# One head's output-projection rows in three DMAs ahead of the last V loads of a two-problem decode-attention kernel

## The chip, the cores and the metric

The kernel runs on one core of a Trainium2 chip. The core has five engines with an instruction stream each: TensorE (PE; its weight loads are listed as PEld), VectorE (DVE), ScalarE (ACT), GpSimd (POOL) and SyncE (SP). SP does no arithmetic here: it issues DMAs, transfers between the chip's memory (HBM) and the core's SBUF. Sixteen DMA engines carry them out. The metric is the device time of one execution in microseconds (us), as a median of several runs; less is better.

## The reference

Two independent problems, A and B, of the same sizes, each one step of attention with a cache and a window. Batch 2, one query token, 32 query heads, 16 key/value heads, head size 128, model width 576. Of 16,384 cached positions the last 4,096 are used.

```python
q = (x @ wq).reshape(B, Sq, Hq, Dh).transpose(0, 2, 1, 3)
k = jnp.repeat(k_cache[:, :, Sk - W:, :], rep, axis=1)      # W = 4096, rep = 2
v = jnp.repeat(v_cache[:, :, Sk - W:, :], rep, axis=1)
scores = jnp.einsum("bhqd,bhkd->bhqk", q, k) * (Dh ** -0.5)
p = softmax(scores, axis=-1)
o = jnp.einsum("bhqk,bhkd->bhqd", p, v)
return o.transpose(0, 2, 1, 3).reshape(B, Sq, Hq * Dh) @ wo
...
jnp.concatenate([a, b], axis=-1)
```

All tensors are bfloat16. The windows of K and V of both problems are 134 MB, wq and wo some 19 MB more; every byte is read once.

## The kernel before

**Staging.** K and V come in slabs of 4,096 KB: 128 partitions of 32 KB, four pairs of batch and key/value head at a time. There are eight slabs of K and eight of V in each problem, 16 pairs (steps) in all. They pass through `ring`, a buffer of four slots (NR = 4). A slab's load (L256) may be issued when the last reader of the slab four places earlier in the order is done: for K the last of the four DVE transposes (L515), for V the last of PE's products with the softmax weights (L631).

**One step.** DVE transposes the K slab in four parts into `xt`, PE multiplies each with the queries (L540), DVE, PE and ACT make the maximum and the exponential, PE multiplies the weights with the V slab into ACC, and ACT copies ACC out. Two steps make a group; the normed head outputs of a group are multiplied with their rows of wo, which lie in the SBUF buffer `wob`. Groups 0 to 3 belong to A, 4 to 7 to B; `proj[7]` is the projection of A's last group.

**The order.** It is written out in Python as lists of operations, one list for each engine; an operation names those that it depends on, and the needed semaphore waits are worked out from that. All loads but one are issued by SP, in the order of `stream`. Its last entries are K of step 13, V of 12, K of 14, K of 15, V of 13, V of 14 and V of 15. An issue that has to wait holds back every later one of SP. A transfer is cut into rows, one packet for each, and each DMA engine works through its own rows in the order of the issues. A load is complete when its semaphore has counted 16.

**The end.** The last slab, V of step 15, is loaded in two pieces (PIECES, L249 to L253) of 96 and 32 of its 128 column blocks, 3,072 KB and 1,024 KB, each with a semaphore of its own. Then `issue_wo(3)` loads the rows of wo for B's last group: 576 KB for step 14 (L291), and through `issue_last` (L272 to L279) the rows of the four heads of step 15. A head has 128 rows of 576 numbers, 1152 bytes each: 144 KB. HEADS, `[(0, 1), (2,), (3,)]`, groups them into three transfers: heads 0 and 1 in one of 288 KB, head 2, head 3. They have the semaphores wl0, wl1 and wl2. Then come the two outputs (L831), of two rows each; A's needs no wait there, B's waits for the end.

PE's work for step 15 after the last piece: the V product, three products whose result is not used, the sum over column blocks (L678), the projection of step 14's heads (L790 with `Rsb`), and that of step 15's heads (L790 with `oTn`), two halves of 288 columns for each head, in the order of HEADS:

```python
parts = [([(oTn[:, h, :], 4 + h) for h in hs], [norm[D_], wo_last[n_]], False, False, n_ == len(HEADS) - 1)
         for n_, hs in enumerate(HEADS)]
```

So the products of heads 0 and 1 wait for DVE's norm (L719) and wl0, those of the next entry for wl1, and the last for wl2. Then ACT and DVE copy the sums into the output row (L822, L823), SP issues the output and waits for it.

Of the kernel before, what the change touches and what calls it, by code (L numbers as in the profile page):

```python
# [59 lines left out]
def build_kernel(nc, probs, out, cfg=None):  # L60
# [8 lines left out]
    NPROB = len(probs)  # L69
# [19 lines left out]
    HH = HD // 2  # L89
# [11 lines left out]
    assert NPROB == 2 and GPP == 4 and NG == 8  # L101
    NSW = 32
    unit_of = {G: u for u, (g0, n) in enumerate(UNITS) for G in range(g0, g0 + n)}
    HEADS = [(0, 1), (2,), (3,)]
    NPC = len(PIECES)

    def by_group(G):
# [6 lines left out]
    with es:  # L114
# [3 lines left out]
        wob = sb("wob", [128, NSW, NOUT], BF16)  # L118
# [62 lines left out]
        x_sem = sem("xload")  # L181
        wl_sem = [sem("wl%d" % n_) for n_ in range(len(HEADS))]
        out_sem = sem("outdone")
# [12 lines left out]
        def dma_op(eng, sem_h, n_dmas, fn, deps, tag):  # L196
            op = S.add(eng, fn, deps, tag)
            dma_count[sem_h] = dma_count.get(sem_h, 0) + 16 * n_dmas
            op.dma = (sem_h, dma_count[sem_h])
            return op  # L200
# [30 lines left out]
        reader = {}  # L231
        wq_dma = {}
        wo_dma = {}
        wo_last = []
        qproj = {}
        proj = {}
        nxt = [0]

        def issue_slab(n):
            kind, D_ = stream[n]  # L240
            if kind == "Q":
                issue_wq(n, D_)
                return
            P, g = D_ // SPP, D_ % SPP
            src_t = probs[P][1] if kind == "K" else probs[P][2]
            src = src_t.rearrange("b h s d -> (b h) s d")[g::SPP, Sk - W:Sk, :].rearrange("c (r j) d -> r c (j d)", r=32)
            r = n % NR
            deps = [reader[n - NR]] if n >= NR else []
            if n == len(stream) - 1:  # L249
                for n_, (ja, jb) in enumerate(PIECES):  # L250
                    def fq(e, n_=n_, ja=ja, jb=jb):
                        return e.dma_start(ring[:, r, ja * 128:jb * 128], src[:, :, ja * 128:jb * 128]).then_inc(piece_sem[n_], 16)  # L252
                    pieces.append(dma_op("sp", piece_sem[n_], 1, fq, deps, "%s%d_q%d" % (kind, D_, n_)))  # L253
                issue_wo(3)
                return
            slab_dma[n] = dma_op("sp", ring_sem[r], 1, lambda e: e.dma_start(ring[:, r, :], src).then_inc(ring_sem[r], 16),  # L256
                                 deps, "%s%d" % (kind, D_))

        def issue_wq(n, P):
            wqP = probs[P][3]  # L260
            r = n % NR
            deps = [reader[n - NR]] if n >= NR else []
            wq_dma[P] = dma_op("sp", wq_sem, 1, lambda e: e.dma_start(
                wqr[:, P, :], wqP[NFC * 128:D, :].rearrange("r (h n) -> r h n", h=2)).then_inc(wq_sem, 16), [], "wqr%d" % P)
            slab_dma[n] = dma_op("sp", ring_sem[r], 1, lambda e: e.dma_start(
                ring[:, r, :], wqP[0:NFC * 128, :].rearrange("(p s) n -> p (s n)", s=NFC)).then_inc(ring_sem[r], 16), deps, "wq%d" % P)

            if P == 0:
                for P_ in range(1, NPROB):
                    x_dma[P_] = load_x(P_, "sp")  # L270

        def issue_last(woP, lo, r0, deps):  # L272
            for n_, hs in enumerate(HEADS):
                def f(e, n_=n_, hs=hs):
                    t, r = divmod(hs[0], 2)
                    row = t * HH + r0 + 256 + 128 * r
                    return e.dma_start(wob[:, lo + 4 + hs[0]:lo + 4 + hs[0] + len(hs), :],
                                       woP[row:row + 128 * len(hs), :].rearrange("(h d) n -> d h n", d=128)).then_inc(wl_sem[n_], 16)
                wo_last.append(dma_op("sp", wl_sem[n_], 1, f, deps, "wl%d" % n_))  # L279

        def issue_wo(part):
            lo, n, r0, P, deps, Gs = (
                (0, 32, 0, 0, [qkeep.get(NG - 1)], (0, 1, 2, 3)),
                (0, 16, 0, 1, [proj.get(3)], (4, 5)),
                (16, 8, 1024, 1, [proj.get(5)], (6,)),
                (24, 4, 1536, 1, [proj.get(7)], (7,)))[part]
            assert None not in deps
            woP = probs[P][4]
            sem_ = wo_sem[lo // 16]
            src = woP.rearrange("(t r) n -> t r n", t=2)[:, r0:r0 + 64 * n, :].rearrange("t (p s) n -> p t (s n)", s=n)  # L290
            op = dma_op("sp", sem_, 1, lambda e: e.dma_start(  # L291
                wob[:, lo:lo + n, :].rearrange("p s n -> p (s n)"), src).then_inc(sem_, 16), deps, "wo%d" % part)
            for G in Gs:
                wo_dma[G] = op
            if part == 3:
                issue_last(woP, lo, r0, deps)

        def issue_until(n_needed):
            while nxt[0] <= n_needed:
                for part in w_at.pop(stream[nxt[0]], []):  # L300
                    issue_wo(part)
                issue_slab(nxt[0])
                nxt[0] += 1
# [462 lines left out]
        def do_proj(D_):  # L766
# [10 lines left out]
            else:  # L777
                parts = [([(oTn[:, h, :], 4 + h) for h in hs], [norm[D_], wo_last[n_]], False, False, n_ == len(HEADS) - 1)
                         for n_, hs in enumerate(HEADS)]
            for lhs, deps, start, rstart, rstop in parts:  # L780
# [146 lines left out]
        for e in ENGS:  # L927
            n = 0
# [63 lines left out]
def bass_concat_heads__sliding_block_cached__sliding_block_cached__decode_kernel(  # L992
    nc, A_x, A_k_cache, A_v_cache, A_wq, A_wo, B_x, B_k_cache, B_v_cache, B_wq, B_wo, out,
):
    build_kernel(nc, [(A_x, A_k_cache, A_v_cache, A_wq, A_wo), (B_x, B_k_cache, B_v_cache, B_wq, B_wo)], out)
# [28 lines left out]
```

## Time and profile before

| | us |
|---|---|
| median of 3 runs (lowest to highest) | 362.61 (362.55 to 362.83) |
| the profiled execution | 363.02 |
| its span, first to last instruction | 361.8 |
| PE busy | 218.6 |
| DVE busy | 200.9 |
| ACT busy | 68.2 |
| POOL busy | 35.3 |
| wo rows of step 14 (L291): issued, landed | 330.1, 358.3 |
| heads 0 and 1 (wl0): issued, landed | 330.7, 359.0 |
| head 2 (wl1): landed | 359.4 |
| head 3 (wl2): issued, landed | 331.9, 359.7 |

The span is the time between the first and the last instruction of the profiled execution. Its whole time is some 1.2 us longer, as the metric includes what lies around the program. No compute engine is busy for more than 60% of the span, while 153.1 MB are read at a mean of 423 GB/s. The end of the profiled execution, in order of time (start, length, engine, line, operation, output and input; in brackets the idle time of the engine before it, and what ended it):

```profile
356.87 0.61 PE L631 MATMUL acc<-ring,pC 128*32 128x512 bf16 x8 [1.01 <-DMA ring<-in_B_v_cache_dram]
...
358.55 0.17 DVE L719 TENSOR_TENSOR oTn<-tb,rsb 128x8 bf16<-128x8 f32 x1 [3.51 <-PE tb L678]
359.07 0.12 PEld L790 LDWEIGHTS st<-wob,oTn 128*2 128x2 bf16 x4 [0.29 <-DVE oTn L719]
359.10 0.94 PE L790 MATMUL st<-wob,oTn 128*2 128x288 bf16 x8
359.40 0.08 PEld L790 LDWEIGHTS st<-wob,oTn 128*2 128x2 bf16 x2 [0.22 <-DMA wob<-in_B_wo_dram]
359.75 0.08 PEld L790 LDWEIGHTS st<-wob,oTn 128*2 128x2 bf16 x2 [0.27 <-DMA wob<-in_B_wo_dram]
360.08 0.40 ACT L822 ACTIVATE pR<-st 2x288 bf16<-2x288 f32 x1 [1.88 <-PE st L790]
```

Besides instructions the trace holds every packet of the DMA engines (start, length, size, queue, but not the engine's number) and the times at which each semaphore was raised. A load of 128 rows raises its semaphore 16 times, once for each DMA engine that is done with its share; such a time is called a mark below. A transfer has landed with its last mark.

### The profile page before, as it was taken

What the parts mean: (1) busy time and instruction counts of PE and PEld (TensorE: products, weight loads), DVE (VectorE), ACT (ScalarE), POOL (GpSimd) and SP (SyncE); (2) the same over time, 40 slices, a digit from 0 to 9 for tenths busy, and PEclk for the clock granted to TensorE, in tenths of its full rate; (3) what the DMA queues carried; (4) which work ended last, traced back from release to release, by engine and by line L of the source; (5) the groups of instructions that cost most, each with busy time, mean ns of one, the idle gap of its engine ahead of it and who ended that gap; (6) DMA issues with size and microseconds to landing.
All of it is one profiled execution on the core that took longest, in us unless ns stands there. A gap on an engine that the chain in (4) does not pass through costs nothing.

```text
span 361.8 us, 2730 instructions
## 1 busy us (share of the span) xinstructions
PE 218.6 (60%) x1318; PEld 55.8 (15%) x945; DVE 200.9 (56%) x175; ACT 68.2 (19%) x149; POOL 35.3 (10%) x55
## 2 busy tenths in 40 slices
PE   0399195763747207466574737766867707657786
PEld 0010021120111101112120201212121201211132
DVE  4112599846647019283756658392919239079931
ACT  1036502130203002103020203020201203002131
POOL 1000000004000400001300040002100040200020
PEclk9999689997889857969698978899898978969999
DMA  8999999999999999999999999999999999999996
GB/s 348 421 449 406 464 406 437 431 408 453 415 442 438 428 424 438 429 428 438 417 446 422 435 428 442 426 435 428 424 424 440 431 424 433 431 438 428 438 409 248
DMA packets 6491, 153.27 MB, mean 424 GB/s; under 512 B 712, under 2 KB 1232, under 8 KB 1616
## 3 DMA queue, kind: packets, MB, share of 16 engines
q1 hardware_dynamic: 6476, 153.10, 98.8%
q8 instruction: 9, 0.15, 0.2%
q14 instruction: 2, 0.02, 0.0%
q10 hardware_dynamic: 4, 0.00, 0.0%
HBM read 153.10 MB, written 0.00 MB: 423 GB/s over the span
## 4 chain that ended last, share of the span: by engine, by line
DMA 72%; DVE 17%; PE 7%; ACT 3%; SPq 1%; issue 0%
DMA ring<-in_B_k_cache_dram 34%; DMA ring<-in_A_k_cache_dram 27%; DVE xt L515 14%; DMA wob<-in_B_wo_dram 8%; DMA wob<-in_B_x_dram 3%; PE st L188 3%; PE st L540 3%; ACT wob L465 1%; DVE wob L475 1%; ACT qk L483 1%; PE st L450 1%; DVE m L550 1%; ACT wob L470 1%; DVE nM L563 0%; SPq L252 0%
## 5 line engine op out<-in xcount | busy, mean ns | idle before, releaser
L515 DVE STREAM_TRANSPOSE xt<-ring 128x2048 f32<-128x2048 f32 x64 | 145.3, 2284 | 86.6 <-DMA ring<-in_A_k_cache_dram 49.8
L540 PE MATMUL st<-xt,zq 128*128 128x512 bf16 x256 | 111.6, 436 | 122.6 <-DVE xt L515 98.1
L188 PE MATMUL st<-xt,zq 128*128 128x512 bf16 x256 | 110.1, 430 | 0.0
L540 PEld LDWEIGHTS st<-xt,zq 128*128 128x128 bf16 x256 | 27.1, 106 | 216.3 <-DVE xt L515 113.5
L631 PE MATMUL acc<-ring,pC 128*32 128x512 bf16 x512 | 32.5, 381 | 1.2 <-DMA ring<-in_B_v_cache_dram 1.2
L568 ACT ACTIVATE nMrep<-nM 1x128 f32<-1x128 f32 x16 | 4.9, 308 | 146.9 <-DVE nM L563 146.9
L643 ACT ACTIVATE acc_sb<-acc 128x512 bf16<-128x512 f32 x16 | 9.5, 596 | 79.9 <-PE acc L631 79.9
L593 DVE STREAM_TRANSPOSE pC<-pR 128x1024 bf16<-128x1024 bf16 x16 | 19.6, 1223 | 3.7 <-ACT pR L585 2.1
L650 POOL TENSOR_TENSOR acc_sb<-acc_sb,masks 128x1024 bf16<-128x1024 bf16 (+1 forms) x8 | 13.4, 1679 | 66.6 <-ACT acc_sb L643 66.6
L550 DVE TENSOR_REDUCE m<-st 128x1 f32<-128x1024 f32 x16 | 19.0, 1190 | 1.4 <-PE st L188 1.4
L502 POOL TENSOR_TENSOR zq<-qk,masks 128x128 bf16<-128x128 bf16 x16 | 6.3, 398 | 136.2 <-PE st L188 114.4
L585 ACT ACTIVATE pR<-st,bias_sb 128x1024 bf16<-128x1024 f32 x16 | 17.8, 1114 | 0.5
L475 DVE STREAM_TRANSPOSE wob<-wob 128x512 f32<-128x512 f32 x8 | 5.7, 711 | 20.3 <-ACT wob L465 12.9
L415 ACT ACTIVATE st<-maskB 128x1024 f32<-128x1024 bf16 x16 | 16.5, 1032 | 1.6 <-POOL rsel L600 0.4
L786 PE MATMUL ot<-wob,Rsb 128*2 128x512 bf16 x56 | 15.2, 390 | 0.0
L631 PEld LDWEIGHTS acc<-ring,pC 128*32 128x32 bf16 x512 | 12.4, 96 | 15.9 <-issue 3.2
L600 POOL TENSOR_TENSOR rsel<-masks,rsum 128x16 f32<-128x16 bf16 x8 | 1.7, 216 | 108.0 <-ACT pR L585 108.0
L188 PE MATMUL tb<-wob,Rsb 128*2 128x64 bf16 x56 | 10.9, 195 | 0.0
L375 PE MATMUL tb<-wob 4*128 4x16 bf16 x5 | 0.3, 179 | 14.5 <-DVE wob L380 14.5
L653 POOL TENSOR_TENSOR acc_sb<-acc_sb 128x512 bf16<-128x512 bf16 (+1 forms) x8 | 8.2, 1029 | 0.6
L188 PE MATMUL st<-ring,wob 128*128 128x512 bf16 x24 | 7.9, 445 | 0.0
L579 ACT ACTIVATE bias_sb<-tb 128x1 f32<-128x1 f32 x16 | 2.7, 171 | 24.8 <-PE tb L573 24.8
(89 smaller groups left out, 99.5 us busy)
## 6 DMA issues: line engine op xcount, KB each, us to landing
ring<-in_A_k_cache_dram SPq DMA_DIRECT2D x8, 4096.0 KB, 30.4
ring<-in_A_v_cache_dram SPq DMA_DIRECT2D x8, 4096.0 KB, 32.5
ring<-in_B_k_cache_dram SPq DMA_DIRECT2D x8, 4096.0 KB, 28.4
ring<-in_B_v_cache_dram SPq DMA_DIRECT2D x7, 4096.0 KB, 32.8
wob<-in_A_wo_dram SPq DMA_DIRECT2D x1, 4608.0 KB, 43.3
ring<-in_A_wq_dram SPq DMA_DIRECT2D x1, 4096.0 KB, 12.7
ring<-in_B_wq_dram SPq DMA_DIRECT2D x1, 4096.0 KB, 22.6
ring<-in_B_v_cache_dram SPq DMA_DIRECT2D x1, 3072.0 KB, 25.5
```

The lines of the kernel that those rows point to most:

```text
L188: return e.add_instruction(mybir.InstMatmult(name=nc.get_next_instruction_name(), engine=i.engine, ins=[e.lower_ap(rhs), i.ins[1]], outs=[ ...
L415: chain[(s, "fill")] = S.add("act", lambda e: e.activation(ST[s % 2][:, :].rearrange("k (h j) -> k h j", h=2), maskB[:].unsqueeze(1).broad ...
L475: chain[(G, "qtr")] = S.add("dve", lambda e: e.transpose(qtr[:].bitcast(FP32), qrow[:].bitcast(FP32)), evs, "qtr%d" % G)
L515: Xop[(s, u)] = S.add("dve", lambda e: e.transpose(xt[:, i % NKT, :].rearrange("k (j w) -> k j w", w=64), ring[:, n % NR, :].bitcast(FP32) ...
L540: first = last = e.matmul(bank, zq[:, p4, s % NZQ, w0:w0 + 128], mv, start=False, stop=stop, skip_group_check=True)
L550: chain[(s, "max")] = S.add("dve", lambda e: e.tensor_reduce(m1[:, 0:1], ST[s % 2][:, :], AX.X, ALU.max), d, "max%d" % s)
L585: chain[(s, "exp")] = S.add("act", lambda e: e.activation(pR[:, :], ST[s % 2][:, :], ACTF.Exp, bias=bias_sb[:, 0:1], scale=SCALE, accum_ou ...
L593: chain[(s, "pC")] = S.add("dve", lambda e: e.transpose(pC[:, s % NPT, :, :].rearrange("k j c -> k (j c)"), pR[:, :]), d, "pC%d" % s)
L631: last = e.matmul(ACC[32 * cb:32 * cb + 32, 0:512], pC[:, D_ % NPT, j0_:j0_ + 4, :].rearrange("k j c -> k (j c)"), ring[:, n % NR, j0_ * 1 ...
L643: acc_ev[D_] = S.add("act", lambda e: e.activation(acc_sb[:, D_ % 2, :], ACC[:, :], ACTF.Copy), d, "accev%d" % D_)
L650: t = S.add("pool", lambda e: e.tensor_tensor(v, v, maskJ[:].unsqueeze(1).unsqueeze(3).broadcast_to([128, l1 - l0, 4, 128]), ALU.mult), [a ...
L786: first = e.matmul(OT[0:Bb, 0:NB0], l_, wob[:, w0 + s_, 0:NB0], start=start and begin, stop=end, skip_group_check=True)
```

## The change

HEADS becomes `[(0, 1), (3,), (2,)]`: the second transfer of step 15's heads is now head 3, the third head 2, and PE multiplies in that order. Head 3's 128 rows are no longer one transfer after V. They come in three, of rows 0 to 14, 14 to 65 and 65 to 128 (SHARES: 14, 51 and 63 rows), and all three are issued before the two pieces of the last V slab. They raise one semaphore, and PE waits until all three have landed. Heads 0 and 1, and then head 2, stay behind the rows of step 14, each as one transfer. The bytes moved and the sums computed are the same.

```diff
-    HEADS = [(0, 1), (2,), (3,)]
+    HEADS = [(0, 1), (3,), (2,)]
+    SHARES = [(0, 14), (14, 65), (65, 128)]
...
-        wo_last = []
+        wo_last = [None] * len(HEADS)
...
             if n == len(stream) - 1:
+                issue_head(1, SHARES, [proj.get(7)])
                 for n_, (ja, jb) in enumerate(PIECES):
...
-        def issue_last(woP, lo, r0, deps):
-            for n_, hs in enumerate(HEADS):
-                def f(e, n_=n_, hs=hs):
-                    t, r = divmod(hs[0], 2)
-                    row = t * HH + r0 + 256 + 128 * r
-                    return e.dma_start(wob[:, lo + 4 + hs[0]:lo + 4 + hs[0] + len(hs), :],
-                                       woP[row:row + 128 * len(hs), :].rearrange("(h d) n -> d h n", d=128)).then_inc(wl_sem[n_], 16)
-                wo_last.append(dma_op("sp", wl_sem[n_], 1, f, deps, "wl%d" % n_))
+        def issue_head(n_, shares, deps):
+            woP, lo, r0 = probs[NPROB - 1][4], 24, 1536
+            hs = HEADS[n_]
+            t, r = divmod(hs[0], 2)
+            row = t * HH + r0 + 256 + 128 * r
+            for pa, pb in shares:
+                def f(e, pa=pa, pb=pb):
+                    return e.dma_start(wob[pa:pb, lo + 4 + hs[0]:lo + 4 + hs[0] + len(hs), :], woP[row:row + 128 * len(hs), :].rearrange(
+                        "(h d) n -> d h n", d=128)[pa:pb]).then_inc(wl_sem[n_], 16)
+                wo_last[n_] = dma_op("sp", wl_sem[n_], 1, f, deps, "wl%d" % n_)
...
             if part == 3:
-                issue_last(woP, lo, r0, deps)
+                issue_head(0, [(0, 128)], deps)
+                issue_head(2, [(0, 128)], deps)
```

## The prediction

> **What bounds the kernel now.** I read the parts in this order: the page's share of DMA, its chain of waits, the same chain in order of time, the DMA engines' share by stretch, and SyncE's own timeline and waits.
>
> ```profile
> DMA  8999999999999999999999999999999999999996
> ...
> q1 hardware_dynamic: 6476, 153.10, 98.8%
> q8 instruction: 9, 0.15, 0.2%
> q14 instruction: 2, 0.02, 0.0%
> ...
> DMA 72%; DVE 17%; PE 7%; ACT 3%; SPq 1%; issue 0%
> ```
>
> The 16 DMA engines are busy from the first slice to the last: 153.1 MB in 361.8 us. Nothing in the change removes a byte, so only the two ends of the stream can move. The end of the chain, in order of time (start, length, what):
>
> ```profile
> 331.87 27.84 DMA wob<-in_B_wo_dram
> 359.71 0.04 issue
> 359.75 0.31 PE st L790 x2
> 360.06 0.02 issue
> 360.08 0.45 DVE pR L823
> ```
>
> The last transfer is issued at 331.9 and lands at 359.71, since all before it on its queue has to go first; after it come two matmuls, a copy and the output. So the end is set by the moment when the *last* of 16 engines finishes the last transfer. The engines by stretch (busy time of PE, PEld, DVE, ACT, POOL, then clock, DMA share, GB/s):
>
> ```profile
> 356.00:357.00 1.00, 0.13 (x4) 0.12 (x8) 0.00 (x0) 0.00 (x0) 0.00 (x0) 1.00 0.99 382
> 357.00:358.00 1.00, 1.00 (x13) 0.11 (x2) 0.00 (x0) 0.46 (x1) 0.00 (x0) 1.00 0.84 311
> 358.00:358.40 0.40, 0.40 (x6) 0.15 (x4) 0.00 (x0) 0.20 (x2) 0.00 (x0) 1.00 0.67 239
> 358.40:358.80 0.40, 0.40 (x10) 0.29 (x9) 0.17 (x1) 0.00 (x0) 0.00 (x0) 1.00 0.55 193
> 358.80:359.20 0.40, 0.40 (x8) 0.12 (x4) 0.00 (x0) 0.00 (x0) 0.00 (x0) 1.00 0.53 168
> 359.20:359.60 0.40, 0.40 (x6) 0.08 (x2) 0.00 (x0) 0.00 (x0) 0.00 (x0) 1.00 0.03 9
> ```
>
> The share falls from 0.99 to 0.53 two microseconds before the end: half of the engines are through while the others still work. The trace marks each engine's end of a transfer. For the last one, head 3's, the 16 marks are, in us: 357.81, .84, .91, .93, 358.01, then 358.36, 358.76, 358.82, then eight from 359.33 to 359.71. Their mean is 358.85: perfect balance would end 0.86 us earlier, and that is all that any shift of rows between engines can give.
>
> Where the lag comes from is in the trace too. The marks of a 4 MB load are 0.5 us apart until 54 us, 1.5 to 1.8 after 65 us, and 1.9 at the end. Each of eight 16 KB instruction packets (q8 above; the ninth comes at 358.81) holds up one engine: a 32 KB row that takes 1.21 us elsewhere takes 1.67 to 1.75 right after seven of them, and the packet before it starts 0.95 to 1.1 late. Linking packets end to start into 16 series, the eight fall on eight different series. Six of these end among the eight late ones; two series can change places where engines run in step, so I take late to mean held up by such a packet.
>
> **The change part by part.** *Issue.* SyncE issues the three parts of head 3 in front of the wait for the last V load:
>
> ```profile
> 306.83 7.44 SPq L256 DMA_DIRECT2D ring<-in_B_v_cache_dram  x2
> 328.85 1.18 SPq L252 DMA_DIRECT2D ring<-in_B_v_cache_dram  x2
> ```
> ```profile
> SPq L252 <- DVE xt L515: 14.6, 1, 14.6
> ```
>
> The second V issue ends at 314.27 and SyncE then waits 14.6 us for the K slot. Three issues of about 0.6 us (L277 took 432 to 597 ns) fit: cost 0. They need PE's projection of problem A's last group; the V issue at 313.7 waited for a later V product of PE, so they wait for nothing. Without that cover they would cost 1.8 us of issue, still 25 us ahead of the landing. One issue (0.5 us) leaves the tail: gain 0, the queue holds 28 us of work. Other engines' instructions keep their order; PE takes heads 0, 1, 3, 2 and so waits for the same number of transfers.
>
> *Rows.* A head is 128 rows of 1152 bytes. In the trace such a packet takes 51 ns and its engine starts the next after 47. Eight rows and a mark are 0.37 us (one engine's marks for the last three transfers: 357.08, 357.45, 357.81). How 14, 51 and 63 rows are dealt out is nowhere in this trace. Bounds: all 128 on one engine, 120 more rows than now, 5.6 us on it; or as even as now, 0. Nearest rows: every transfer shown has equal shares on the engines that it uses, 8 of 128, 16 of 256, 1 of 2 (the 2-row output has only two engines' marks). Equal shares of 51 on at most 16 engines mean 3 engines of 17 (or 1 of 51), of 63 at most 9 of 7, of 14 at most 14 of 1. I take these largest counts, since 128 and 256 rows use all 16, and let the smaller groups lie inside the larger, the two-row engines among them (a choice; other nestings are B and C below): three engines carry 25 rows of head 3 (17 more than now, +0.80 us), six carry 8 (0), five carry 1 (-0.33), two carry none (-0.37).
>
> [...]
>
> *What the marks become.* The first output transfer has 2 rows and is queued right behind. Its packets follow those of an early engine (end of last packet 357.42) and of a middle one (358.41, mark about 358.82). If these two are among the three, they end at 358.7 and 358.82 + 0.80 + 0.01 for two more marks = 359.63. The late eight end between 359.33 and 359.71, or 0.33 to 0.37 less where they lose rows. Last mark: 359.63, if the latest ones lose rows and the third loaded engine isn't late: -0.08.
>
> *What lies behind.* V's last piece lands later where rows were put in front: +1.18 on the loaded three (the middle one ends piece 2 at 355.9, so 357.1), +0.38 on six, at most +0.01 to +0.05 on the others; its last mark goes from 356.83 to at most 357.2. PE then starts up to 0.38 later and the last norm ends at 359.10 in place of 358.72. That is covered by the wait for heads 0 and 1, whose last mark is now one transfer (0.37) ahead of the end: 359.26. In the kernel before it is 358.97 and PE starts at 359.07. So PE starts heads 0, 1, 3 at 359.36, six products at (0.66 - 0.29)/7 = 0.053 us, the spacing of the eight on L790 for the earlier rows: 359.68. Head 2 is ready at 359.67. PE is 0.01 late; with the 0.31 us of the last two products it ends at 359.99 to 360.0, from 360.06.
>
> *Sum.* 361.8 - 0.06 = 361.7 us of span. Around the span lie 363.02 - 361.8 = 1.2 us in the profiled execution, which is 0.41 above the median 362.61; so the forecast is 362.61 - 0.06 = 362.55, and its own range 362.4 to 362.7 (0.15 us of gain if the middle engine carries less, a mark or two more than counted).
>
> **The rivals.** *A, slower: the ninth instruction packet.* It starts at 358.81 and today harms nobody: the eight engines spared so far are through by then. With 17 more rows the middle engine works until 359.2. A packet on it costs from 0.6 (16 KB at the 1.21 us of 32 KB) to 1.55 us (what the eighth cost: 1.00 on the mark, 0.54 on the next row), of which 0.08 is slack: +0.5 to +1.45, 363.1 to 364.05, mostly over 363.35. It decides if the packet falls on a loaded engine that still has rows. For it: eight packets, eight engines, so the next is likely one of the eight others; against: only two or three of these are still at work.
>
> *B, slower by less: the third loaded engine is a late one.* Then the last mark is 359.33 + 0.81 to 359.71 + 0.81, or +0.43 to +0.81: 363.05 to 363.4. Eight of the 14 engines not identified are late; but late ones may also cluster, and I can't tell numbers from this trace.
>
> *C, faster: the middle engine is not among the loaded.* The late eight lose rows and end by 359.38, early engines with 17 more rows at 358.8: -0.33, of which PE gives back some 0.1: 362.3 to 362.4. Against: two-row transfers used that engine. If instead a late one is among the six unchanged, nothing is gained, which is inside the forecast.
>
> *D, it does not spread.* One engine for 51 or 128 rows: +1.3 to +5.6. Against: equal shares seen everywhere.
>
> *E, small transfers pay a fixed price.* One transfer becomes three, the smallest 16 KB. The only transfer on an empty queue, the output, is issued by 360.83 and marked at 361.70: 0.87 us. Two more of those, not overlapped, are +1.7: 364.3. Against: the last marks of the last three transfers are 358.97, 359.36 and 359.71, so 144 KB cost 0.35 to 0.39 behind each other, with nothing fixed to be seen.
> [...]
>
> **How the numbers follow.** Forecast 0.56, A 0.13, B 0.14, C 0.09, D 0.03, E 0.02; 0.03 is kept for what none of them names. 0.2% is 0.73 us, about what a measurement of this kernel can tell from no change: 361.88 to 363.34. A is over that bound in 0.11 of its 0.13, B in 0.02, D and E wholly: slower 0.18. No case is 0.73 us faster, as balance itself gives 0.86 and this dealing reaches half, so faster has the 0.03 alone. Same 0.79. Range 362.2 to 363.5: forecast, C and B, 0.79, and 0.03 of A.
>
> **What would show it.** Three issues between 314 and 317 on SyncE; 14, 3 and 9 marks for the three parts; the DMA share over 357 to 359.2 flatter than 0.84, 0.67, 0.55, 0.53; the last mark at 359.6; V's last piece at 357.2 at most; the chain still ending in the wob transfer and L790's successor. Wrong if an engine's last rows show a stall near 358.8 (A), if three engines end alone after 360 (B), or if the chain ends in PE's products and not in a transfer.

## The result and the profile after

The change makes the kernel slightly slower. Measured in alternation on the same chip, the kernel after takes 363.47 us (median of 18 runs, 363.24 to 364.25), the kernel before 362.85 (18 runs, 362.55 to 363.15): a ratio of 1.0021, with a 95% interval of 1.0014 to 1.0027, which is 0.5 to 1.0 us. The forecast was 0.06 us faster. The measured time lies inside the predicted range, but it has gone the other way than the forecast. The profiled execution after takes 363.34 us with a span of 362.1 (before: 363.02 and 361.8).

From the page of after: the share of the DMA engines in 40 slices, the queue of the loads, and the chain's shares by engine.

```profile
DMA  8999999999999999999999999999999999999996
...
q1 hardware_dynamic: 6486, 153.10, 98.8%
...
DMA 72%; DVE 16%; PE 8%; ACT 3%; SPq 0%; issue 0%
```

The bytes are the same, 153.10 MB, the queue's packets take the same share of the DMA engines' time as before, 98.8%, and ten packets came to the queue (6,476 before; marks are packets of their own). Nothing here shows a loss. The end of the chain of waits of after, in order of time (start, length, what):

```profile
329.04 28.42 DMA ring<-in_B_v_cache_dram
357.50 0.62 PE acc L636 x8
...
359.14 1.24 PE st L795 x16
```

Before, the chain's last transfer was the one of head 3's rows. Now it is V's last piece, and PE's products follow it to the end. The end of after, in order of time (columns as in the profile before; L636, L724, L795 and L827 are what L631, L719, L790 and L822 were):

```profile
357.50 0.62 PE L636 MATMUL acc<-ring,pC 128*32 128x512 bf16 x8 [0.30 <-DMA ring<-in_B_v_cache_dram]
...
359.18 0.17 DVE L724 TENSOR_TENSOR oTn<-tb,rsb 128x8 bf16<-128x8 f32 x1 [2.45 <-PE tb L683]
359.69 0.40 PEld L795 LDWEIGHTS st<-wob,oTn 128*2 128x2 bf16 x8 [0.28 <-DVE oTn L724]
359.72 0.65 PE L795 MATMUL st<-wob,oTn 128*2 128x288 bf16 x8
360.41 0.40 ACT L827 ACTIVATE pR<-st 2x288 bf16<-2x288 f32 x1 [1.58 <-PE st L795]
```

V's last piece lands at 357.46 (before 356.83), the norm is ready at 359.35, and PE starts the last heads at 359.69. The profile names the norm as what ended that wait, but the norm had been done for 0.34 us; the last mark of heads 0 and 1 is at 359.58 (before 358.97), so it was that transfer. Then all eight products run without a stop, since the very last transfer, head 2, has landed at 359.96 (before 359.71). That the chain above gives PE everything behind V's last piece comes from the same wrong name.

The end is 0.33 us later than before in the two profiles, but the two executions were not level when the change began. The mean mark of V of step 13, the last slab that is through before any row of head 3 moves, was 335.99 in after and 336.35 in before, a difference that began near 70 us and has nothing to do with the change. Taken from there, the last marks are 0.61 us later and the end 0.69, which agrees with the 0.62 of the medians.

So the loss lies between V of step 13 and V's first piece, where head 3's rows now are. A part of it is already in V of step 14, directly in front of them: its mean mark is 346.24 (before 346.16), 0.44 us later when the head start is taken off. SP's timeline of after (start, length, instruction) shows three issues in front of the pieces of V, as predicted, and the 12.6 us of waiting behind them that hide them:

```profile
307.09 7.44 SPq L258 DMA_DIRECT2D ring<-in_B_v_cache_dram  x2
314.57 1.23 SPq L281 DMA_DIRECT2D wob<-in_B_wo_dram  x3
328.45 1.20 SPq L254 DMA_DIRECT2D ring<-in_B_v_cache_dram  x2
```

Head 3's semaphore then counts 26 marks between 345.05 and 347.73, which is the 14 + 3 + 9 of the prediction. In that stretch the windows differ. Before, by stretch (busy time of PE, PEld, DVE, ACT, POOL, then granted clock, DMA share, GB/s):

```profile
344.00:348.00 4.00, 3.02 (x47) 1.29 (x51) 1.67 (x3) 2.17 (x5) 1.26 (x2) 1.00 0.96 406
```

The same stretch of after:

```profile
344.00:348.00 4.00, 2.08 (x27) 0.99 (x31) 1.39 (x2) 1.86 (x4) 1.87 (x3) 0.93 0.96 313
```

The DMA share is 0.96 in both, and the bytes per second fall from 406 to 313 GB/s: the engines are just as busy and move less. The lengths of single packets tell the rest. Packets of after in this stretch (start and length in ns, bytes):

```
344694 1755 32768
344827 1766 32768
344686 1301 24576
344705 1333 24576
345161   99  1152
345083   82  1152
```

The last rows of V of step 14 (32 KB) took mostly 1.74 to 1.77 us, against 1.22 before, the first rows of V's first piece (24 KB) 1.30 to 1.35 against 0.91, and head 3's rows 62 ns on average against 51. One engine that carries none of head 3's rows (its last row of V of step 14 is followed at once by its first of 24 KB) had 24 KB rows of 1333, 1238 and 1009 ns and lost 0.83 us. So the slowing is not confined to the engines that carry head 3's rows.

As a measure that the experiments share, I take the step from the mean mark of V of step 13 to the mean mark of V's first piece. It was 17.10 us before. Head 3's rows in front of the piece must add eight rows and a mark (in the trace of before 47 ns for a row and 9 for a mark), 0.38, so 17.48 is due. It was 18.33: a loss of 0.85 us. Each step below is from one profile, but it repeats well: five kernels below that leave this part as it was have 17.10 to 17.12.

### The profile page after: what moved, and what is told of

It is laid out like the page before. It is cut to its first block, busy times and chain, and to the rows that moved or that the text cites. A ratio compares the mean times of both kernels' runs of the same rounds, so it can differ in the third digit from the quotient of the medians.

```text
span 362.1 us, 2730 instructions
## 1 busy us (share of the span) xinstructions
PE 223.0 (62%) x1316; PEld 57.0 (16%) x945; DVE 200.9 (55%) x175; ACT 68.3 (19%) x149; POOL 35.3 (10%) x55
## 3 DMA queue, kind: packets, MB, share of 16 engines
q1 hardware_dynamic: 6486, 153.10, 98.8%
HBM read 153.10 MB, written 0.00 MB: 423 GB/s over the span
## 4 chain that ended last, share of the span: by engine, by line
DMA 72%; DVE 16%; PE 8%; ACT 3%; SPq 0%; issue 0%
DMA ring<-in_B_k_cache_dram 33%; DMA ring<-in_A_k_cache_dram 27%; DVE xt L520 14%; DMA ring<-in_B_v_cache_dram 8%; DMA wob<-in_B_wq_dram 4%; PE st L189 4%; PE st L545 3%; ACT wob L470 1%; DVE wob L480 1%; ACT qk L488 1%; PE st L455 1%; DVE m L555 1%; ACT wob L475 1%; DVE nM L568 0%; PE st L795 0%
## 5 line engine op out<-in xcount | busy, mean ns | idle before, releaser
L636 PE MATMUL acc<-ring,pC 128*32 128x512 bf16 x512 | 36.1, 410 | 1.4 <-DMA ring<-in_B_v_cache_dram 1.4
L636 PEld LDWEIGHTS acc<-ring,pC 128*32 128x32 bf16 x512 | 13.2, 101 | 18.6 <-issue 7.3
## 6 DMA issues: line engine op xcount, KB each, us to landing
ring<-in_A_wq_dram SPq DMA_DIRECT2D x1, 4096.0 KB, 12.6
```

Of the source, the lines that this page charges most:

```text
L636: last = e.matmul(ACC[32 * cb:32 * cb + 32, 0:512], pC[:, D_ % NPT, j0_:j0_ + 4, :].rearrange("k j c -> k (j c)"), ring[:, n % NR, j0_ * 1 ...
```

## The experiments

The theories. **S**: each engine normally writes its own partitions, and rows that go to the partitions of other engines make the engines wait. **U**: the shares are unequal, which brings the engines out of step. **P**: small rows among V's large ones are what is slow, wherever they go. **N**: the number of transfers is. Which engine writes which partition no run shows, nor how many rows cross in this sense: the packets and marks tell only how many rows an engine has, 8 of 128. Where S expects a number below, that is the author's estimate. The edits on head 3 are against the kernel after.

**One transfer.** Head 3 stays in front of V, with all 128 partitions in one transfer.

```diff
-    SHARES = [(0, 14), (14, 65), (65, 128)]
+    SHARES = [(0, 128)]
```

> Head 3's rows in front of the last V slab as one transfer of 128 rows. The step is the mean mark of V's first piece of step 15 minus the mean mark of V of step 13: 17.11 us in the kernel before, 18.33 in the changed one, of which 0.38 is the eight rows an engine that were put in between. Theory S (rows that an engine writes to partitions which other engines normally write make all engines wait): nothing crosses here, the step is 17.5 and the time that of before within 0.15 us. Theory U (unequal numbers of rows bring the engines out of step): also 17.5 and no change. Theory P (a head's small rows among the large ones of V cost it, however dealt): the step stays near 18.3 and the time 0.6 us above before. Theory N (three transfers where there was one): 17.5 and no change.

Measured: 363.01 us against 362.78 of the kernel before in the same comparison (which the next three share), ratio 1.0003 (0.9994 to 1.0012). The step is 17.49, a loss of 0.01. The same stretch of this kernel:

```profile
344.00:348.00 4.00, 2.51 (x35) 1.12 (x35) 1.39 (x2) 2.17 (x5) 1.54 (x3) 0.94 1.01 420
```

The full rate, with the same small rows between V's large ones: P falls. The move in front of V costs nothing that can be told from noise (the interval is -0.2 to +0.4 us), the division does.

**Two halves of the partitions.** By equal shares, as the trace of before shows them on 16 engines for 128 and 256 rows (8 and 16 on each), every engine has four rows of each half.

```diff
-    SHARES = [(0, 14), (14, 65), (65, 128)]
+    SHARES = [(0, 64), (64, 128)]
```

> [...] Theory S: the step (17.11 before, 18.33 changed) is 17.7 to 18.1, the time 0.2 to 0.5 us above before. Theory U: step 17.5, no change of time. Theory N: a third to a half of the loss, as there is one transfer more and not two: step 17.9, +0.3. So U is told from S, and N from neither.

Measured: 363.40 us, ratio 1.0013 (1.0005 to 1.0022); step 17.95, a loss of 0.46 although by equal shares every engine has as many rows as before, eight of the head. The stretch:

```profile
344.00:348.00 4.00, 2.93 (x44) 1.28 (x47) 1.67 (x3) 2.17 (x5) 1.26 (x2) 1.00 0.97 352
```

U falls, at least as the whole cause.

**Three thirds of the columns.** Three transfers again, but each over all 128 partitions and 192 of the 576 columns.

```diff
-    SHARES = [(0, 14), (14, 65), (65, 128)]
+    SHARES = [(0, 192), (192, 384), (384, 576)]
...
-                    return e.dma_start(wob[pa:pb, lo + 4 + hs[0]:lo + 4 + hs[0] + len(hs), :], woP[row:row + 128 * len(hs), :].rearrange(
-                        "(h d) n -> d h n", d=128)[pa:pb]).then_inc(wl_sem[n_], 16)
+                    return e.dma_start(wob[:, lo + 4 + hs[0]:lo + 4 + hs[0] + len(hs), pa:pb], woP[row:row + 128 * len(hs), :].rearrange(
+                        "(h d) n -> d h n", d=128)[:, :, pa:pb]).then_inc(wl_sem[n_], 16)
...
-                issue_head(0, [(0, 128)], deps)
-                issue_head(2, [(0, 128)], deps)
+                issue_head(0, [(0, 576)], deps)
+                issue_head(2, [(0, 576)], deps)
```

> Head 3's rows in front of the last V slab in three transfers of all 128 rows and a third of the columns each (384 bytes a row). [...] Theory S and U: step 17.5 to 17.7 (three times as many rows, at perhaps 20 ns each, are 0.5 us in place of 0.38), time within 0.2 us of before. Theory N: three transfers of 48 KB cost as in the changed kernel, step 18.3, +0.6 us. Theory P: step 18.3 or more.

Measured: 362.92 us, ratio 1.0000 (0.9991 to 1.0009); step 17.57. Three times as many rows (of 384 bytes, 22 ns each) and as many transfers as in the change, for 0.09 us on the step: N falls, and with it the rival E of the prediction, a fixed price for small transfers.

**A whole slab in two halves of the partitions.** If S is right, the effect must be large where all 16 engines write into 64 partitions for long. The kernel before, with V of step 6 as two transfers:

```diff
+            if kind == "V" and D_ == 6:
+                def f2(e):
+                    e.dma_start(ring[0:64, r, :], src[0:16]).then_inc(ring_sem[r], 16)
+                    return e.dma_start(ring[64:128, r, :], src[16:32]).then_inc(ring_sem[r], 16)
+                slab_dma[n] = dma_op("sp", ring_sem[r], 2, f2, deps, "%s%d" % (kind, D_))
+                return
```

> The kernel before, with one 4,096 KB slab in mid-stream (V of step 6) as two transfers of partitions 0 to 63 and 64 to 127. Every engine moves the same bytes in rows of the same size as before. Theory S: in each half 16 engines write to the partitions of eight, so this slab runs at down to half the rate: up to 9.7 us more (half of the 9.7 us for a slab would be the least), time +4 to +10 us. Theories U, N and P: nothing unequal, no small rows, one transfer more: time within 0.3 us of before.

Measured: 374.0 us, ratio 1.0304 (1.0288 to 1.0319), 11.2 us for one of the 16 slabs of V, more than the 4 to 10 that were expected. In the stretch of that slab, before:

```profile
174.00:190.00 16.00, 12.04 (x68) 3.00 (x52) 11.50 (x10) 2.71 (x5) 1.61 (x4) 0.79 1.01 434
```

and with the halves:

```profile
174.00:190.00 16.00, 10.28 (x36) 2.24 (x20) 11.96 (x10) 2.71 (x5) 0.62 (x2) 0.71 0.97 203
```

A 32 KB row takes 2.55 us in place of 1.22, a little more than twice as long, and the DMA share still reads 0.97. Both halves were dealt to all 16 engines: the loads' queue has 16 packets more (6,492, before 6,476), one mark for each engine.

**The same slab in two halves of the columns.** The edit is shown against the partition halves.

```diff
-                    e.dma_start(ring[0:64, r, :], src[0:16]).then_inc(ring_sem[r], 16)
-                    return e.dma_start(ring[64:128, r, :], src[16:32]).then_inc(ring_sem[r], 16)
+                    e.dma_start(ring[:, r, 0:8192], src[:, :, 0:8192]).then_inc(ring_sem[r], 16)
+                    return e.dma_start(ring[:, r, 8192:16384], src[:, :, 8192:16384]).then_inc(ring_sem[r], 16)
```

> The control to the slab in two halves of partitions (11.2 us more): the same slab in two transfers of all 128 partitions and half of the columns. All theories that blame the crossing of partitions: 0 within 0.2 us. If a second transfer for a slab costs by itself: up to 11 us.

Measured: 363.03 us against 362.88 (which the next three share), ratio 1.0003 (0.9994 to 1.0012), at 444 GB/s:

```profile
174.00:190.00 16.00, 11.27 (x68) 2.90 (x52) 11.15 (x10) 3.31 (x6) 2.18 (x4) 0.89 1.04 444
```

Dividing this large transfer by columns costs nothing that can be told; dividing it by partitions does.

**Thirds by equal shares: 16, 48 and 64 rows.** By equal shares each engine again gets eight rows, one, three and four of each part.

```diff
-    SHARES = [(0, 14), (14, 65), (65, 128)]
+    SHARES = [(0, 16), (16, 64), (64, 128)]
```

> [...] Theory U (unequal shares are what costs): step 17.5, time that of before.

Measured: 363.41 us, ratio 1.0016 (1.0007 to 1.0024); step 18.05, a loss of 0.56, where U expected none. The stretch:

```profile
344.00:348.00 4.00, 2.51 (x32) 1.08 (x36) 1.55 (x3) 2.17 (x5) 0.78 (x2) 1.00 0.99 350
```

The two halves, these thirds and the change lost 0.46, 0.56 and 0.85 us on the step: the loss does not come from the inequality of the shares alone, which is nil in the first two. The whole times of the three don't tell them apart (ratios of 1.0013, 1.0016 and 1.0021 with intervals that overlap).

**Two heads divided.** Head 2 is treated as head 3, all six parts in front of V.

```diff
                 issue_head(1, SHARES, [proj.get(7)])
+                issue_head(2, SHARES, [proj.get(7)])
...
-                issue_head(2, [(0, 128)], deps)
```

> Heads 3 and 2 both in front of the last V slab, each in transfers of 14, 51 and 63 rows; heads 0 and 1 are the last transfer. Theory S: twice the rows and twice the loss, step 17.10 + 2 x 0.38 + 2 x 0.84 = 19.5 us, time 1.1 to 1.6 us above before. If the loss is one disturbance that does not grow with the rows (engines out of step once): step 18.7, time +0.6 us.

Measured: 365.01 us, ratio 1.0059 (1.0045 to 1.0072), 2.1 us slower. The step is 19.04, where two heads' rows make 17.86 due: a loss of 1.18, 1.4 times that of one head and not twice, so the expectation of 19.5 was too high, while the 1.1 to 1.6 us that were expected for the time were too low. The end of this kernel's chain of waits:

```profile
329.37 29.60 DMA ring<-in_B_v_cache_dram
359.02 0.61 PE acc L636 x8
...
360.66 1.23 PE st L795 x16
```

V's last piece lands at 358.97, but here too the chain gives PE too much. The norm is ready at 360.87, the last transfer, now heads 0 and 1, has its last mark at 361.08, and PE starts the last heads at 361.19. Counted from V of step 13, that last mark is 1.47 us later than the last one of before. The mean of its marks is 1.16 later, close to the loss of the step, and the other 0.31 come from a wider spread, 2.43 us for 1.90. After it PE has eight products to run and not two, 0.79 us in place of 0.35. Together these are 1.91 of the 2.1 us. By the dealing of the change (14, 3 and 9 marks, 17 rows more on three engines) the loaded engines now carry 34 rows more, an estimate, so the wider spread is likely the inequality of U; no run with equal shares for two heads tests that.

**Divided, but behind V.** The three parts come after the rows of heads 0 and 1, where no V rows are left to be slowed.

```diff
             if n == len(stream) - 1:
-                issue_head(1, SHARES, [proj.get(7)])
...
                 issue_head(0, [(0, 128)], deps)
+                issue_head(1, SHARES, deps)
                 issue_head(2, [(0, 128)], deps)
```

> Head 3's three transfers of 14, 51 and 63 rows behind heads 0 and 1, with head 2 as the last transfer, so that all of wo comes after V as in the kernel before. Theory S: the step is back at 17.1, but the rows cost the same behind V: head 2's last mark is 0.3 to 0.8 us later than the 359.71 of before, time +0.3 to +0.8 us. Theory that the place among the large V rows is needed for the loss: last mark within 0.1 us of 359.71 and no change of time.

Measured: 363.44 us, ratio 1.0013 (1.0004 to 1.0022). The step is 17.11, as in the kernel before, so V's first piece is untouched, and the loss has moved along with the rows: head 2's last mark is 360.25, 0.54 us later than the last mark of before (0.38 counted from V of step 13), inside what S expected. In the microsecond from 357 on, where the share and the rate of before were 0.84 and 311:

```profile
357.00:358.00 1.00, 0.85 (x11) 0.23 (x10) 0.00 (x0) 0.19 (x1) 0.00 (x0) 1.00 0.99 280
```

More busy and fewer bytes again: rows of 4,608 bytes for step 14's heads take up to 291 ns here and 181 elsewhere. P falls a second time.

**Where from, or where to?** In the partition halves the place read in HBM and the place written in SBUF went together. Two runs set them apart, beside a kernel before of 362.84; both edits are shown against the partition halves. In the first, the two transfers read what the halves read, one after the other, but each writes all 128 partitions.

```diff
-                    e.dma_start(ring[0:64, r, :], src[0:16]).then_inc(ring_sem[r], 16)
-                    return e.dma_start(ring[64:128, r, :], src[16:32]).then_inc(ring_sem[r], 16)
+                    raw = src_t.rearrange("b h s d -> (b h) s d")[g::SPP, Sk - W:Sk, :].rearrange("c (q j) d -> q c (j d)", q=64)
+                    e.dma_start(ring[:, r, 0:8192], raw[0:32]).then_inc(ring_sem[r], 16)
+                    return e.dma_start(ring[:, r, 8192:16384], raw[32:64]).then_inc(ring_sem[r], 16)
```

> The kernel before with the V slab of step 6 in two transfers that read what the two partition halves read (first row blocks 0 to 15 of the four heads, then 16 to 31, 2,048 KB each) but write all 128 partitions: each 32 KB row is cut into two of 16 KB, the first transfer fills the first half of the columns of all partitions, the second the other half. Step 6's V lies in another order in the buffer than its weights, so the sums of that step's heads are not the reference's. The partition halves cost 11.2 us, and in them the place of the reads in HBM and the place of the writes in SBUF varied together. S (the cost comes from the partitions written): within 0.3 us of the kernel before, as the column halves (+0.25), with rows of 16 KB at about 0.62 us. Rival R (the cost comes from reading only one half of each head's window at a time, or from a read place that other engines normally read): +9 to +12 us, and rows of 16 KB at about 1.2 us.

Measured: 362.84 us, ratio 0.9999 (0.9989 to 1.0008), rows of 16 KB at 0.61 us:

```profile
174.00:190.00 16.00, 11.56 (x68) 2.91 (x52) 11.38 (x10) 3.03 (x6) 1.19 (x3) 0.81 1.03 440
```

In the second, each transfer writes one half of the partitions and reads from the whole window.

```diff
-                    e.dma_start(ring[0:64, r, :], src[0:16]).then_inc(ring_sem[r], 16)
-                    return e.dma_start(ring[64:128, r, :], src[16:32]).then_inc(ring_sem[r], 16)
+                    e.dma_start(ring[0:64, r, :], src[0::2]).then_inc(ring_sem[r], 16)
+                    return e.dma_start(ring[64:128, r, :], src[1::2]).then_inc(ring_sem[r], 16)
```

> The mirror image: the same slab in two transfers, partitions 0 to 63 and 64 to 127, each of which reads every second row block of the four heads, so that each transfer's reads lie over the whole window. Step 6's V again lies in another order than its weights. S: +10.5 to +11.9 us as the partition halves, rows of 32 KB at about 2.5 us. R with the half window as cause: within 0.5 us of the kernel before. R with the unusual read place as cause would give the loss here too, but then in the other run as well.

Measured: 373.72 us, ratio 1.0301 (1.0285 to 1.0316), rows of 32 KB at 2.50 us:

```profile
174.00:190.00 16.00, 9.63 (x36) 2.14 (x20) 11.72 (x10) 2.71 (x5) 1.27 (x3) 0.79 0.99 211
```

The loss goes with the partitions written and not with the place read, and the rival R falls. For the large slab this is shown. Whether a row costs more because its partitions are those of another engine, or because 16 engines share too few partitions, these runs don't separate. That the small rows of the change lose by the same cause is carried over from it, with the runs on head 3 in its favour: every division by partitions lost (0.46, 0.56 and 0.85 us on the step), the one by columns lost 0.09 there and nothing in the whole time (ratio 1.0000).

## Why the prediction was wrong, step by step

**The step that failed is the price of the moved rows.** The prediction said that nothing in the change removes a byte, so only the ends of the stream can move, and it priced a row of head 3 at 47 ns on the engine that carries it and at nothing on all others but for the marks (+0.01 to +0.05 us). No reason was given for that nothing. In its place the runs show a cost that reaches engines without such a row: 0.85 us on the mean mark of V's first piece, of which 0.61 are left on the last marks. The sum of that step was to be -0.08 us on the last mark. No rival had this mechanism either, and none of A to E happened as described. How many rows cross no run shows, so S gives no sum to hold against these losses. Spread over all the rows that were moved (the loss times 16 engines, divided by 128 rows), they are an estimate of 0.11 us of engine time a row in the change, 0.07 in the equal thirds and 0.06 in the two halves, where a row takes 47 ns; the 11.2 us of the slab of step 6 are 1.4 us a row, where a row takes 1.22. What stays open is the engine without a single row of head 3. In the simplest form of S, where a row delays only the engine whose partition it takes, and by its own time, an engine with eight partitions (128 by 16) loses at most 8 x 47 ns = 0.38 us. It lost 0.83.

**What balance could give was sized by the wrong engines.** The prediction let the latest engines be those that lose rows, which was its condition for a gain. Following the packets into 16 series (those that run in step can be mixed up in this) shows eight late ones in after: three carry eight rows of head 3 as before (seven of the third part and one of the first), four carry one row, and one carries none. Late engines that kept their eight rows would have set the end as before. So even without the loss nothing would have been gained; this was named as a part of the forecast, and as one of its unproved choices. The last marks are spread over 1.62 us in place of 1.90, and over a later time.

**The order at PE** came out as the sum had it, only later. In the sum PE waits for heads 0 and 1 (359.26), runs six products and reaches head 2 when that has just landed. Measured, heads 0 and 1 came at 359.58 (with the head start of 0.36 us a delay of 0.97 from 358.97, of which 0.37 is the planned move of one transfer towards the end), and PE then ran its eight products in one go. From the last mark to the end of the products it took 0.41 us in place of 0.35: the 0.06 beside the 0.61. The prediction had named a chain that ends in PE's products as a sign that would make it wrong. That sign contradicts its own sum, in which PE comes to head 2 after it has landed, and it says nothing about the loss: with one transfer, where nothing was lost, the chain ends in the same way.

```profile
357.43 0.61 PE acc L636 x8
...
359.07 1.25 PE st L795 x16
```

**Right were** the cost of the issues (nothing: three of them in 1.23 us, with 12.6 us of waiting left), the dealing of the rows (14, 3 and 9 marks), and that the ninth instruction packet does no harm: it came at 359.41, took 1.05 us, and no mark is late by it. V's last piece was to land by 357.2 and did at 357.46, or 357.82 without the head start, 0.62 beyond that bound: again the loss. The DMA share over the end became flatter, as the prediction wanted it, for the wrong reason. From the windows of after:

```profile
357.00:358.00 1.00, 0.70 (x9) 0.12 (x8) 0.00 (x0) 0.00 (x0) 0.00 (x0) 1.00 1.01 393
358.00:358.40 0.40, 0.40 (x7) 0.11 (x2) 0.00 (x0) 0.23 (x1) 0.00 (x0) 1.00 0.67 245
358.40:358.80 0.40, 0.35 (x2) 0.00 (x0) 0.00 (x0) 0.40 (x2) 0.00 (x0) 1.00 0.81 291
358.80:359.20 0.40, 0.40 (x9) 0.26 (x9) 0.02 (x1) 0.03 (x1) 0.00 (x0) 1.00 0.61 213
359.20:359.60 0.40, 0.40 (x8) 0.17 (x4) 0.15 (x1) 0.00 (x0) 0.00 (x0) 1.00 0.41 125
```

1.01, 0.67, 0.81, 0.61 and 0.41 stand where 0.84, 0.67, 0.55, 0.53 and 0.03 were. A part of this is better balance (1.62 us of spread for 1.90), and a part is that the same work arrives 0.6 us later.

No version here beats the kernel before. One transfer in front of V and the column thirds can't be told from it (ratios of 1.0003 and 1.0000, each give or take 0.0009).

## What to carry to other kernels

As far as these runs go: let every transfer span all 128 partitions, and divide it by columns where it must be divided (a slab in two halves of the partitions cost 11.2 us, in two halves of the columns 0.15, which is within the noise). A count of rows for each DMA engine is no cost model as long as it leaves out which partitions are written (two halves with equal counts lost 0.46 us on the step). The busy share of the DMA engines did not show such a loss (0.96 at 406 and at 313 GB/s, 0.97 at 203), so read the bytes per second and the lengths of single packets beside it. And before a few rows are moved to shift the end of a stream, make sure which engines end last.

## What the runs showed of the hardware that was not expected

**An engine's time depends on where others write.** Sixteen engines that wrote into 64 partitions ran at about half the rate, 203 and 211 GB/s (the partition halves with either place of reading) against 434, at a DMA share of 0.97 and 0.99. And in after, the engine that had none of head 3's rows lost 0.83 us while the others wrote theirs.

**An issue can block for 11 to 13 us.** In after, SP needs 11.53 us for two issues, 10.89 of them for the second alone, where the two take 1.1 us in the kernels with one transfer, two halves or equal thirds. SP's timeline of after:

```profile
330.34 11.53 SPq L281 DMA_DIRECT2D wob<-in_B_wo_dram  x2
```

and of the column thirds, where the second issue takes 13.13:

```profile
330.05 13.77 SPq L281 DMA_DIRECT2D wob<-in_B_wo_dram  x2
```

With two heads divided the issue of V's last piece takes 13.19 us, and with the parts behind V three issues take 2.58, 8.15 and 8.90. What these four have in common is that at least one engine has more small packets queued than in the others, 16 to 34 rows by the dealing above, which is an estimate; why an issue then takes so long no run shows. It cost nothing here, as the transfers wait some 29 us in the queue anyway, but an issue that another engine's start hangs on would have been late.
